# Reordering the first stage of a fused attention and MLP kernel, and the first two block products of its later groups

## The chip, the cores and the metric

The kernel runs on one core of a Trainium2 chip. The time is device time in microseconds, the median of several runs. A profile is one more execution, recorded by the hardware profiler; times inside it count from its first instruction. PE is the matrix engine, with PEld its weight loads; DVE, ACT and POOL are the vector, scalar and GpSimd engines; SP issues most DMAs. Each engine works through its own instructions in order and waits on semaphores for the others.

## The reference

Blockwise linear attention with a decay per head feeds a two-layer MLP with a norm and a residual:

```python
for b in range(nb):                       # 12 blocks of 64 rows, 4 batches, 8 heads of 64
    intra = einsum('bhic,bhjc->bhij', qb, kb) * Dmask
    intra = einsum('bhij,bhjd->bhid', intra, vb)
    inter = einsum('bhid,bhde->bhie', qb * lam_pow, kv_state)
    out[:, :, sl] = intra + inter
    kv_state = lam_block * kv_state + einsum('bhsd,bhse->bhde', kb * rev_pow, vb)
x = out.transpose(0, 2, 1, 3).reshape(4, 768, 512)
xn = (x - mean(x)) / sqrt(var(x) + 1e-6) * g_ln
return x + relu(xn @ w_ch1) @ w_ch2       # w_ch1 512x2048, w_ch2 2048x512
```

## The kernel before

**Windows.** The 3072 rows are cut into 12 windows u of 256 rows; window u belongs to batch u mod 4. A window has a first and a second 128-row chunk, `ab` = 0 and 1. k(u), q(u) and v(u), 512 KB each, are loaded by SP (L76); window 0's in two halves. `in_k` (L215, L231) casts k to bf16, `in_q_one(u, engine, j)` (L236) casts half j of q and scales it, `in_v` (L242) does so for v into `vb`. `transpose_pe(u, a, pairs)` (L250) turns k (a=0) or q (a=1) on PE into `kqT`; DVE or ACT copies it out of PSUM (L251). `scores` (L273), `mask` on DVE (L283), `kv` (L307), `new_state`, `av` (L419) and `inter` (L432) are the attention; `norm` (L465 to L470) reads the result `po` and leaves the centred `xc`; `keep_x` (L475) copies `po` to `x`; `to_xT(u, ab)` (L493) transposes `xc`; `rstd_of` (L506) makes the scale that is used only where the MLP's result is added. `sqrt_first` is a small activation that makes ACT load its square root table early.

**The MLP.** Each window is a group g of two 128-row tiles. Layer 1 takes W1 in four pieces `w1[c]` of 512 columns, layer 2 takes W2 in four pieces `w2[c]` of 512 rows; both are loaded and cast by DMAs that POOL issues (`load_w1` L117, `load_w2` L120). `m1a.tile(0, i)` and `m1b.tile(0, i)` (L640) apply W1(0) to one tile of group 0 or 1; `m1s(m1a, c, lo, hi)` (L530) applies halves of piece c to both tiles. Each result passes ReLU on ACT into `hT` (L533, L643). Groups 0 to 3 use the plain layer 2 (`m2`, L666, ended by `finish` L690). Groups 4 to 11 use seven products of half-size blocks (`m2w`, L624), with sums of W2 blocks (`w_sums`) and of hT blocks (`h_sums`, L548 to L550) made on DVE. A product has 8 multiplies r = 0 to 7 (L565) and adds into a PSUM bank; `evict` reads a bank when its product is complete.

**The order.** It is written out by hand; a step's instructions go to each engine's queue in the order in which the steps stand. `behind(tile)` (L727) is a one-column copy on POOL: it makes all that POOL issues after it wait for the DMA of that tile. `open_in(u, True)` writes one column of the k tile from POOL (L91), and SP's load of k(u) waits for it, with all that SP issues later. `mm_tile` gives one of four PSUM banks, the one free for longest. `units(n)` runs the next n entries of a plan: the rest of group 1's layer 1, then layer 2 of groups 0 and 1, then the later groups.

In the first stage (L736 to L998) POOL's steps stand in this order:

```python
    behind(qkv_in[0]["k"][:, 0, 0, 0:1]); load_w1(0); in_k(0, nc.gpsimd, HB)
    in_v(0, nc.gpsimd, HA); in_v(0, nc.gpsimd, HB)
    behind(qkv_in[1]["k"][:, 0, 0, 0:1]); load_w1(1); load_w1(2)
    in_q_one(1, nc.gpsimd, 0); in_q_one(1, nc.gpsimd, 1); load_w1(3); load_w2(0)
    in_v(1, nc.gpsimd); behind(w1[2][:, 0, 0:1]); open_in(2, True)
    behind(w2[0][:, 0, 0:1]); load_w2(1); load_w2(2)
    in_q_one(2, nc.gpsimd, 0); in_q_one(2, nc.gpsimd, 1); load_w2(3); in_v(2, nc.gpsimd); open_in(3, True)
```

PE's in the same stage, after `inter(0, 0)`: k(1)'s transposes, xT(0,0), inter(0,1), tile a(0,0), xT(0,1), q(1)'s transposes, tile a(0,1), scores of window 1, one m1 step, kv(1), two m1 steps, av(1), inter(1,0), m1, inter(1,1), m1, xT(1,0), m1, xT(1,1), tiles b(0,0) and b(0,1).

Of the kernel before, what the change touches and what calls it, by code (L numbers as in the profile page):

```python
# [12 lines left out]
ACT = mybir.ActivationFunctionType  # L13
# [4 lines left out]
def kernel(  # L18
# [97 lines left out]
    def load_w1(c):  # L116
        nc.gpsimd.dma_start(w1[c], moe_w_ch1[:, c * W1C:(c + 1) * W1C].rearrange("(k p) f -> p k f", p=128))  # L117
# [115 lines left out]
    def in_q_one(u, eng, j):  # L233
        src = qkv_in[u]["q"].rearrange("p (a e) j d -> p a e j d", e=2)
        lq = (lam_q[:, :, j] if u < LB else lam_p[:, 0, :]).rearrange("p (a e) -> p a e", e=2)
        eng.tensor_tensor(part(1, st[u]["kq"], ALL)[:, :, :, j], src[:, :, :, j],  # L236
                          lq[:, :, :, None].to_broadcast([128, NP, 2, D]), op=ALU.mult)

    def in_v(u, eng, hs=ALL):
        n = hs.stop - hs.start  # L240
        lv = lam_v[:, hs, :, None] if u < LB else lam_p[:, 1, hs, None, None]
        eng.tensor_tensor(st[u]["vb"][:, hs], qkv_in[u]["v"][:, hs], lv.to_broadcast([128, n, 2, D]), op=ALU.mult)  # L242
# [272 lines left out]
    def mlp(g):  # L515
# [38 lines left out]
        def product(i, bank, part, first):  # L554
            if first:
                pr[bank] = mm_tile([128, DM // 2], F32, f"pw{bank}")
            w, h = DM // 2, blocks()
            lhs = dict(P1=lambda r: h[:, r, 0], P2=lambda r: h[:, r, 2], P3=lambda r: hs["4"][:, r], P4=lambda r: h[:, r, 3],
                       P5=lambda r: hs["13"][:, r, 1], P6=lambda r: hs["2"][:, r], P7=lambda r: hs["13"][:, r, 0])[i]
            org = dict(P1=(0, 0), P2=(1, 0), P3=(1, 1)).get(i)  # L560
            own = dict(P5=0, P6=1, P7=2, P4=3).get(i)
            for r in part:
                c, k = divmod(r, W2K // 2)
                rhs = wt[c][:, k, own] if org is None else w2[c][:, 2 * k + org[0], org[1] * w:(org[1] + 1) * w]
                nc.tensor.matmul(pr[bank], lhsT=lhs(r), rhs=rhs, start=(first and r == 0), stop=(r == KB // 2 - 1),  # L565
                                 skip_group_check=True)
# [3 lines left out]
        def evict(i):  # L570
            u = g
            x, rstd = x_keep[u]
            w = DM // 2
            r = [rstd[:, ab:ab + 1] for ab in range(2)]
            xq = [[x[:, ab, z * w:(z + 1) * w] for z in range(2)] for ab in range(2)]

            def scaled(out, in0, ab, in1):
                nc.vector.scalar_tensor_tensor(out, in0=in0, scalar=r[ab], in1=in1, op0=ALU.mult, op1=ALU.add)  # L578

            def tmp(name):  # L580
                ev[name] = wk.tile([128, w], F32, tag="ev_" + name, bufs=1, name="ev_" + name)
                return ev[name]

            if i == "P1":
                o_of[u] = x
            o = o_of[u]
            oq = [[o[:, ab, z * w:(z + 1) * w] for z in range(2)] for ab in range(2)]
            if i == "P1":
                nc.scalar.activation(tmp("u1"), pr["a"], ACT.Identity, scale=r[0])  # L589
                nc.gpsimd.tensor_tensor(oq[0][0], ev["u1"], xq[0][0], op=ALU.add)  # L590
            elif i == "P2":
                scaled(oq[0][0], pr["b"], 0, oq[0][0])
                if u == NU - 1:
                    for j in range(2):
                        nc.sync.dma_start(rows_of(u)[j][:, 0, 0:w], o[half[j], 0, 0:w])
            elif i == "P7":
                nc.scalar.activation(tmp("p7"), pr["c"], ACT.Identity, scale=r[1])
                nc.gpsimd.tensor_tensor(xq[1][1], ev["p7"], xq[1][1], op=ALU.add)  # L598
            elif i == "P5":
                scaled(xq[1][1], pr["d"], 1, xq[1][1])  # L600
            elif i == "P6":
                scaled(o[:, 1].rearrange("p (z w) -> p z w", z=2), pr["a"][:, None, :].to_broadcast([128, 2, w]), 1,
                       x[:, 1].rearrange("p (z w) -> p z w", z=2))
                last_rows(1, 1)
                scaled(oq[0][1], pr["a"], 0, xq[0][1])
            elif i == "P4":
                scaled(oq[1][0], pr["c"], 1, oq[1][0])
                last_rows(1, 0)
            elif i == "P3":
                scaled(oq[0][1], pr["d"], 0, oq[0][1])  # L610
                last_rows(0, 1)

        def last_rows(ab, z):
# [4 lines left out]
            for j, eng in enumerate((nc.sync, nc.scalar)):  # L618
# [2 lines left out]
        products = (("P1", "a", True), ("P2", "b", True), ("P7", "c", True), ("P5", "d", True),  # L621
                    ("P6", "a", False), ("P4", "c", False), ("P3", "d", False))

        def m2w(n):  # L624
            lo, hi = 7 * n, 7 * n + 7
            for q, (i, bank, first) in enumerate(products):
                part = [r for r in range(8) if lo <= 8 * q + r < hi]
                if part:
                    product(i, bank, part, first and part[0] == 0)
                    if part[-1] == 7:  # L630
                        evict(i)

        def m1_tile(c, i):
            nonlocal hT
# [114 lines left out]
    for i in range(2):  # L749
        nc.scalar.activation(lam_p[:, i], lnlam, ACT.Exp, scale=e_p[:, i:i + 1])  # L750
    in_q(0, nc.vector, HA)
    behind(qkv_in[0]["k"][:, 0, 0, 0:1])
    load_w1(0)
    in_k(0, nc.gpsimd, HB)
    in_q(0, nc.vector, HB)
    transpose_pe(0, 1, (0, 1))
    transpose_pe(0, 0, (2, 3), nc.vector)
# [184 lines left out]
    in_k(1, nc.scalar)  # L942
    norm(0, 0, early=True)
    reader(0)
    behind(qkv_in[1]["k"][:, 0, 0, 0:1])
    load_w1(1)
    load_w1(2)
    in_q_one(1, nc.gpsimd, 0)
    in_q_one(1, nc.gpsimd, 1)
    load_w1(3)  # L950
    load_w2(0)
    in_v(1, nc.gpsimd)
    behind(w1[2][:, 0, 0:1])
# [12 lines left out]
    transpose_pe(1, 1, (0, 1), nc.vector)
    transpose_pe(1, 1, (2, 3))
    m1a.tile(0, 1)
    keep_x(0, nc.vector.tensor_copy)
    nc.scalar.activation(sqrt_first, eps_t, ACT.Sqrt)  # L970
    scores(1, 0)
    scores(1, 1, early=True)
    mask(1, 0)
    mask(1, 1)
    m1s(m1a, 1, 0, 1)
    kv(1, "sc")
    new_state(1, 0, nc.scalar)
    m1s(m1a, 1, 1, 2)
    rstd_of(0)
    m1s(m1a, 2, 0, 1)  # L980
    av(1, (0, 1))
    av(1, (2, 3))
    inter(1, 0)
    norm(1, 0, early=True)
    m1s(m1a, 2, 1, 2)
    inter(1, 1)
    norm(1, 1, early=True)
    st[1]["tmp"] = state_sum(1, 1)
    m1s(m1a, 3, 0, 1)
    to_xT(1, 0)  # L990
    m1s(m1a, 3, 1, 2)
    to_xT(1, 1)
    open_window(2)
    in_k_one(2, nc.vector, 0)
    in_k_one(2, nc.vector, 1)
    m1b.tile(0, 0)
    m1b.tile(0, 1)
    keep_x(1, nc.scalar.copy)  # L998
    rstd_of(1)
    behind(w2[0][:, 0, 0:1])  # L1000
    load_w2(1)
    load_w2(2)
    in_q_one(2, nc.gpsimd, 0)
    in_q_one(2, nc.gpsimd, 1)
    load_w2(3)
    in_v(2, nc.gpsimd)
    open_in(3, True)
    load_in(3, "k", nc.sync)
    load_in(3, "q", nc.sync)
# [347 lines left out]
```

## Time and profile before

| | |
|---|---|
| median of 3 runs | 210.56 us (210.29, 210.56, 211.72) |
| span of the profiled execution | 209.7 us |
| PE busy | 198.0 us, 94% |
| DVE, ACT, POOL busy | 137.1, 120.1, 85.1 us |
| layer 1, L530 | 736 multiplies, 84.8 us |
| W1 and W2 pieces | 8 DMAs of 512 KB each as written, 9.2 us from issue to landing (median) |
| loads of a whole k, q, v | 512 KB each, 6.2 to 8.2 us |

The page's picture of the span in 40 slices, each digit a tenth of busy time in that slice:

```profile
PE   2989599999999999999999999999999999999992
POOL 4746338229638240617255441781284202011020
DMA  4999999999899998992898998897978020058403
```

A slice is 5.2 us. PE is below nine tenths in the first, third, fifth and last slices alone (2, 8, 5, 2); the DMA engines are full from the second slice on for most of the run.

### The profile page before, as it was taken

Reading aid. Unit: us, or ns where it says so; the run is one execution under the profiler, and the core shown is the slowest. Engines: PE = TensorE matmul, PEld = TensorE weight load, DVE = VectorE, ACT = ScalarE, POOL = GpSimd, SP = SyncE. Lnnn points to the kernel's source line nnn. Section 1 sums busy time; section 2 is a strip of 40 time slices with the busy share of each in tenths; the row PEclk is TensorE's granted clock in tenths of the full one; section 3 lists DMA queues with packets and bytes.
Section 4 is the critical chain, followed back from the end, with each engine's and each line's share of the span. In section 5 each row is a group of like instructions: output and inputs, shape, how many; then the busy total and the mean of one; then the engine's idle time right before and its main releaser. Section 6 shows DMA issues by size and latency. Waiting matters only on the chain.

```text
span 209.7 us, 7231 instructions
## 1 busy us (share of the span) xinstructions
PE 198.0 (94%) x3099; PEld 156.6 (75%) x3099; DVE 137.1 (65%) x277; ACT 120.1 (57%) x277; POOL 85.1 (41%) x116
## 2 busy tenths in 40 slices
PE   2989599999999999999999999999999999999992
PEld 0469479645685577578888888888888888888881
DVE  2677481437575966749798775778777947865253
ACT  4764668516155468438666775485596575652620
POOL 4746338229638240617255441781284202011020
PEclk9999999999999999999999999999999999999998
DMA  4999999999899998992898998897978020058403
GB/s 121 294 270 211 206 276 167 196 306 273 159 322 201 218 184 159 194 271 55 177 226 124 187 204 155 201 208 109 226 134 185 6 50 3 18 125 279 137 14 88
DMA packets 91042, 36.39 MB, mean 174 GB/s; under 512 B 65153, under 2 KB 88193, under 8 KB 91010
## 3 DMA queue, kind: packets, MB, share of 16 engines
q1 hardware_dynamic: 86400, 31.53, 70.2%
q0 software_dynamic: 4224, 4.19, 12.6%
q8 instruction: 24, 0.39, 0.9%
q10 hardware_dynamic: 386, 0.20, 0.4%
q14 instruction: 8, 0.07, 0.1%
HBM read 27.27 MB, written 6.29 MB: 160 GB/s over the span
## 4 chain that ended last, share of the span: by engine, by line
PE 76%; DMA 7%; issue 7%; SPq 3%; DVE 3%; POOL 2%; POOLq 0%; ACT 0%; ACTq 0%; DVEq 0%
PE pm L530 34%; PE pm L666 14%; DMA vin<-in_v_dram 7%; PE pwa L565 6%; PE pwd L565 5%; PE pwc L565 5%; SPq L76 3%; PE pwb L565 2%; PE po L419 2%; PE po L432 1%; PE sc L273 1%; DVE x L578 1%; PE po L406 1%; PE sc L353 1%; PE pk L307 1%
## 5 line engine op out<-in xcount | busy, mean ns | idle before, releaser
L530 PE MATMUL pm<-xT,w 128*128 128x256 bf16 x736 | 84.8, 273 | 0.0
L530 PEld LDWEIGHTS <-w 128*128 128x128 bf16 x736 | 70.4, 98 | 9.5 <-DVE Smid L388 0.3
L533 ACT ACTIVATE hT<-pm 128x512 f16<-128x512 f32 x92 | 53.8, 598 | 28.8 <-PE pm L530 28.5
L666 PE MATMUL pm<-w,hT 128*128 128x512 f16 x128 | 30.2, 380 | 0.0
L565 PEld LDWEIGHTS <-hs 128*128 128x128 f16 x256 | 24.9, 98 | 2.9
L313 POOL TENSOR_TENSOR Sn<-Stmp,lam_s 128x256 bf16<-128x256 f32 x16 | 9.8, 615 | 42.1 <-DVE Stmp L317 23.6
L590 POOL TENSOR_TENSOR x<-ev_u,x 128x256 f32<-128x256 f32 x8 | 6.5, 816 | 45.0 <-ACT ev_u L589 45.0
L548 DVE TENSOR_TENSOR hs<-hT 128x1024 f16<-128x1024 f16 x16 | 12.8, 802 | 16.0 <-ACT hT L533 16.0
L565 PEld LDWEIGHTS <-hT 128*128 128x128 f16 x192 | 18.1, 98 | 3.6 <-ACT hT L533 1.6
L666 PEld LDWEIGHTS <-hT 128*128 128x128 f16 x128 | 11.7, 98 | 12.1
L283 DVE TENSOR_TENSOR mA<-sc,keep 128x512 bf16<-128x512 f32 x20 | 13.1, 684 | 7.0 <-PE sc L273 7.0
L458 ACT ACTIVATE x<-po 128x512 f32<-128x512 f32 x18 | 10.6, 590 | 9.7 <-PE po L419 5.3
L460 DVE SCALAR_TENSOR_TENSOR xc<-po,nmean,g_row 128x512 bf16<-128x512 f32 x18 | 12.9, 745 | 4.7 <-ACT nmean L459 4.7
L242 POOL TENSOR_TENSOR vb<-vin,lam_v 128x1024 bf16<-128x1024 f32 (+1 forms) x7 | 11.6, 1656 | 4.1 <-DMA vin<-in_v_dram 4.0
L503 ACT ACTIVATE sq<-x,nmean 128x512 bf16<-128x512 f32 x18 | 12.9, 719 | 0.3
L242 POOL TENSOR_TENSOR vb<-vin,lam_p 128x1024 bf16<-128x1024 f32 x6 | 11.9, 1985 | 2.5 <-DMA vin<-in_v_dram 2.5
L578 DVE SCALAR_TENSOR_TENSOR x<-pwd,rstd,x 128x256 f32<-128x256 f32 x16 | 7.7, 483 | 7.8 <-POOL x L598 7.8
L236 POOL TENSOR_TENSOR kq<-qin,lam_q 128x512 bf16<-128x512 f32 x10 | 10.3, 1045 | 5.6 <-DMA qin<-in_q_dram 5.6
L550 DVE TENSOR_TENSOR hs<-hs,hT 128x512 f16<-128x512 f16 x16 | 10.1, 628 | 0.6
L494 ACT COPY xT<-xt 128x512 bf16<-128x512 bf16 x10 | 5.8, 582 | 7.7 <-PE xt L493 7.7
L236 POOL TENSOR_TENSOR kq<-qin,lam_p 128x512 bf16<-128x512 f32 x9 | 9.3, 1042 | 1.3 <-PE pwc L565 1.2
L578 DVE SCALAR_TENSOR_TENSOR x<-pwa,rstd,x 128x512 f32<-128x512 f32 (+1 forms) x16 | 9.1, 613 | 0.8
(129 smaller groups left out, 300.4 us busy)
## 6 DMA issues: line engine op xcount, KB each, us to landing
out_dram<-x SPq DMA_DIRECT2D x22, 256.0 KB, 3.8
w<-in_moe_w_ch_dram POOLq DMA_DIRECT2D x8, 512.0 KB, 9.2
kin<-in_k_dram SPq DMA_DIRECT2D x14, 256.0 KB, 4.8
qin<-in_q_dram SPq DMA_DIRECT2D x14, 256.0 KB, 4.9
vin<-in_v_dram SPq DMA_DIRECT2D x14, 256.0 KB, 5.2
kin<-in_k_dram SPq DMA_DIRECT2D x5, 512.0 KB, 6.2
qin<-in_q_dram SPq DMA_DIRECT2D x5, 512.0 KB, 8.2
vin<-in_v_dram SPq DMA_DIRECT2D x5, 512.0 KB, 8.1
```

What stands on the lines that cost most here:

```text
L236: eng.tensor_tensor(part(1, st[u]["kq"], ALL)[:, :, :, j], src[:, :, :, j], lq[:, :, :, None].to_broadcast([128, NP, 2, D]), op=ALU.mult)
L242: eng.tensor_tensor(st[u]["vb"][:, hs], qkv_in[u]["v"][:, hs], lv.to_broadcast([128, n, 2, D]), op=ALU.mult)
L283: nc.vector.tensor_tensor(s[f"mA{hf}"][:, e], s[f"sc{hf}"][e], kp[:, None, :, :].to_broadcast([128, 2, 2, 128]), op=ALU.mult)
L458: nc.scalar.activation(x, po, ACT.Copy, accum_out=sm)
L460: nc.vector.scalar_tensor_tensor(xc, in0=po, scalar=nm, in1=g_row, op0=ALU.add, op1=ALU.mult)
L503: nc.scalar.activation(sq, s["x"][:, ab], ACT.Square, bias=s["nmean"][:, ab:ab + 1], accum_out=ss[:, ab:ab + 1])
L530: nc.tensor.matmul(pm[:, b, :], lhsT=w1[n // W2K][:, kk, (n % W2K) * 128:(n % W2K + 1) * 128], rhs=xT_of[g][:, kk, 0:N], start=(b == 0 and ...
L533: nc.scalar.activation(hT[:, u * NB:(u + 1) * NB, 0:N], pm, ACT.Relu)
L548: nc.vector.tensor_tensor(s13, b[:, :, 1:2, :].to_broadcast([128, n, 2, 128]), b[:, :, 0:4:3, :], op=ALU.subtract)
L565: nc.tensor.matmul(pr[bank], lhsT=lhs(r), rhs=rhs, start=(first and r == 0), stop=(r == KB // 2 - 1), skip_group_check=True)
L578: nc.vector.scalar_tensor_tensor(out, in0=in0, scalar=r[ab], in1=in1, op0=ALU.mult, op1=ALU.add)
L666: nc.tensor.matmul(acc[i], lhsT=hT[:, kk, i * 128:(i + 1) * 128], rhs=w2[kk // W2K][:, kk % W2K, :], start=(kk == 0), stop=(kk == KB - 1))
```

## The change

Five edits, all of order, but for two POOL copies that go (`behind` of k(0) and of k(1)) and some copies that move from one engine to another.

In the first stage POOL casts k(0) ahead of W1(0), and the W1 pieces stand between the casts of window 1. W2(0) goes behind the gate of window 2's loads; window 2's q casts go ahead of W2(1), its v ahead of W2(3). PE's order, q(1)'s transposes and the scores first, changes with it; q(1)'s transposes are copied out by ACT alone, and `keep_x(0)` moves from DVE to ACT. The table load and both `rstd_of` move past the second scores of window 2. In `m2w` the first two products take turns by seven multiplies.

```diff
+        early = [(q, r) for q in (0, 1) for r in range(7)] + [(0, 7), (1, 7)]
+        order = early + [(q, r) for q in range(2, 7) for r in range(8)]
+
         def m2w(n):
-            lo, hi = 7 * n, 7 * n + 7
-            for q, (i, bank, first) in enumerate(products):
-                part = [r for r in range(8) if lo <= 8 * q + r < hi]
-                if part:
-                    product(i, bank, part, first and part[0] == 0)
-                    if part[-1] == 7:
-                        evict(i)
+            for q, r in order[7 * n:7 * n + 7]:
+                i, bank, first = products[q]
+                product(i, bank, [r], first and r == 0)
+                if r == 7:
+                    evict(i)
...
     in_q(0, nc.vector, HA)
-    behind(qkv_in[0]["k"][:, 0, 0, 0:1])
+    in_k(0, nc.gpsimd, HB)
     load_w1(0)
-    in_k(0, nc.gpsimd, HB)
     in_q(0, nc.vector, HB)
...
     reader(0)
-    behind(qkv_in[1]["k"][:, 0, 0, 0:1])
+    in_q_one(1, nc.gpsimd, 0)
     load_w1(1)
+    in_q_one(1, nc.gpsimd, 1)
     load_w1(2)
-    in_q_one(1, nc.gpsimd, 0)
-    in_q_one(1, nc.gpsimd, 1)
+    in_v(1, nc.gpsimd)
     load_w1(3)
-    load_w2(0)
-    in_v(1, nc.gpsimd)
     behind(w1[2][:, 0, 0:1])
     open_in(2, True)
     load_in(2, "k", nc.sync)
     load_in(2, "q", nc.sync)
     load_in(2, "v", nc.sync)
+    load_w2(0)
     transpose_pe(1, 0, (0, 1), nc.vector)
     transpose_pe(1, 0, (2, 3), nc.vector)
     to_xT(0, 0)
     inter(0, 1)
     norm(0, 1, early=True)
     st[0]["tmp"] = state_sum(0, 1)
+    transpose_pe(1, 1, (0, 1))
+    transpose_pe(1, 1, (2, 3))
     m1a.tile(0, 0)
     to_xT(0, 1)
-    transpose_pe(1, 1, (0, 1), nc.vector)
-    transpose_pe(1, 1, (2, 3))
+    scores(1, 0)
+    mask(1, 0)
+    scores(1, 1, early=True)
+    mask(1, 1)
+    keep_x(0, nc.scalar.copy)
     m1a.tile(0, 1)
-    keep_x(0, nc.vector.tensor_copy)
-    nc.scalar.activation(sqrt_first, eps_t, ACT.Sqrt)
-    scores(1, 0)
-    scores(1, 1, early=True)
-    mask(1, 0)
-    mask(1, 1)
-    m1s(m1a, 1, 0, 1)
     kv(1, "sc")
     new_state(1, 0, nc.scalar)
-    m1s(m1a, 1, 1, 2)
-    rstd_of(0)
-    m1s(m1a, 2, 0, 1)
+    m1s(m1a, 1, 0, 1)
     av(1, (0, 1))
     av(1, (2, 3))
     inter(1, 0)
     norm(1, 0, early=True)
-    m1s(m1a, 2, 1, 2)
+    m1s(m1a, 1, 1, 2)
     inter(1, 1)
     norm(1, 1, early=True)
     st[1]["tmp"] = state_sum(1, 1)
+    m1s(m1a, 2, 0, 1)
+    to_xT(1, 0)
+    m1s(m1a, 2, 1, 2)
     m1s(m1a, 3, 0, 1)
-    to_xT(1, 0)
+    to_xT(1, 1)
     m1s(m1a, 3, 1, 2)
-    to_xT(1, 1)
     open_window(2)
     in_k_one(2, nc.vector, 0)
     in_k_one(2, nc.vector, 1)
+    in_q_one(2, nc.gpsimd, 0)
+    in_q_one(2, nc.gpsimd, 1)
     m1b.tile(0, 0)
     m1b.tile(0, 1)
     keep_x(1, nc.scalar.copy)
-    rstd_of(1)
     behind(w2[0][:, 0, 0:1])
     load_w2(1)
     load_w2(2)
-    in_q_one(2, nc.gpsimd, 0)
-    in_q_one(2, nc.gpsimd, 1)
+    in_v(2, nc.gpsimd)
     load_w2(3)
-    in_v(2, nc.gpsimd)
     open_in(3, True)
...
-    units(1)
+    units(2)
     transpose_pe(2, 0, (0, 1, 2, 3))
-    units(2)
+    units(1)
     transpose_pe(2, 1, (0, 1, 2, 3))
...
     units(2)
     s2(2)
+    nc.scalar.activation(sqrt_first, eps_t, ACT.Sqrt)
+    rstd_of(0)
+    rstd_of(1)
     units(2)
     s0(2)
```

More of the change, by code (lines that the diff above doesn't have):

```diff
@@ L1031, in units @@
             f(*a)
+    units(2)
+    transpose_pe(2, 0, (0, 1, 2, 3))
     units(1)
-    transpose_pe(2, 0, (0, 1, 2, 3))
-    units(2)
     transpose_pe(2, 1, (0, 1, 2, 3))
```

## The prediction

> **What bounds the kernel now.** I read the page first: TensorE (PE) is busy 94% of a 209.7 us span, so only its idle time is for sale. The table of stretches says where that is (columns: time and number of instructions for PE, weight loads, DVE, ACT, POOL, then clock, DMA share, GB/s):
>
> ```profile
> 22.00:24.16 2.16, 0.00 (x0) 0.02 (x1) 1.32 (x3) 1.06 (x3) 1.95 (x2) 1.00 1.24 207
> 31.00:186.00 155.00, 154.97 (x2505) 122.03 (x2503) 107.34 (x205) 94.14 (x223) 66.97 (x82) 1.00 0.86 169
> ```
>
> From 31 us to 186 us PE has no gap (the modelled ends touch), and one hole, 2.16 us, stands at 22 us. Whatever PE gains before 31 us reaches the end, as long as nothing behind it comes late. The timeline of PE names the hole and its pace:
>
> ```profile
> 15.84 1.86 PE L640 MATMUL pm1t<-xT,w 128*128 128x128 bf16 x16 [0.32 <-ACT xT L494]
> 20.94 1.05 PE L530 MATMUL pm<-xT,w 128*128 128x256 bf16 x8
> 24.16 0.44 PE L307 MATMUL pk<-vb,kq 64*64 64x64 bf16 x32 [2.17 <-POOL vb L242]
> 30.94 1.95 PE L640 MATMUL pm1t<-xT,w 128*128 128x128 bf16 x32
> ```
>
> The hole waits for vb of window 1. Also, 16 multiplies take 1.86 us at 15.84 and 32 of the same take 1.95 us at 30.94: single records start 107 ns apart until 19.9 us, 56 ns after it. The early stage runs at half pace. Why vb is late, from POOL's timeline:
>
> ```profile
> 5.40 0.94 POOL L117 DMA_DIRECT2D w<-in_moe_w_ch_dram  x1
> 11.38 1.56 POOL L117 DMA_DIRECT2D w<-in_moe_w_ch_dram  x2
> 15.62 2.05 POOL L236 TENSOR_TENSOR kq<-qin,lam_q 128x512 bf16<-128x512 f32 x2 [2.68 <-DMA qin<-in_q_dram]
> 22.21 1.90 POOL L242 TENSOR_TENSOR vb<-vin,lam_v 128x1024 bf16<-128x1024 f32 x1 [3.05 <-DMA vin<-in_v_dram]
> ```
>
> POOL waits for q(1) until 15.6 and for v(1) until 22.2, although SP issued both by 9.3 us. The DMA queues by stretch, 3 to 9.5 us and then 9.5 to 13.5 us (packets, MB, share):
>
> ```profile
> q1 hardware_dynamic: 3750, 1.87, 109.6%
> ```
> ```profile
> q0 software_dynamic: 514, 0.51, 76.6%
> q1 hardware_dynamic: 861, 0.43, 44.1%
> ```
>
> q1 is SP's loads, q0 the weight pieces. Alone, q1 moves 1.87/6.5 = 0.288 MB/us; beside W1(0) it falls to 0.43/4 = 0.11. W1(0), issued at 5.40, first moves after 9.5. Last, the chain of waits, for the block products:
>
> ```profile
> 99.39 0.97 PE pwa L565 x8
> 100.36 0.87 PE pwb L565 x8
> ```
>
> Eight groups open with such a 0.97; the groups of instructions put 1.6 us, 8 times, of weight loads waiting for the last hT against them.
>
> **Part 1: W1(0) behind in_k(0).** The copy at 5.15 goes; POOL's casts of k stay at 6.95 (they wait for k) and end at 7.87; W1(0) issues 7.87 to 8.8, in the 0.93 us in which POOL waited for v anyway. So 2.5 us later. Its first packets came 3.5 us after the end of the issue (6.34, 9.9; W1(1): 12.20, some 15.6), so now about 12.3. Until then q1 is undisturbed: the loads up to q(1) are 2.62 MB, from 2.8 us at 0.288, so 11.9; completion counted 1.2 us later, as for k(0) (0.26 MB by 3.7, seen at 5.1): q(1) at 13.2 instead of 15.54. Bounds: 12.6, and 15.5 if W1(0) cuts in as it does now.
>
> The Trainium skill, DMA: Bandwidth & Descriptors, Specifications, gives the first byte of a gpsimd-issued DMA about 1 us, and its section on queues has each DMA engine take turns between queues packet by packet. By that W1(0) would move at 9.8 us, q(1) would come as late as now, and the kernel would take about 209.8. The row (3.5 us, twice) speaks for 12.3, and I go by the row.
>
> **Part 2: the new POOL order.** A cast of q half takes 1.04, a weight issue 0.81, vb 1.90. q cast 13.2 to 14.25, W1(1) to 15.05, q cast to 16.1, W1(2) to 16.9, then v(1). Behind the new first wait stand both W1 pieces, vb, W1(3) and the gate of window 2's loads. v(1) and W1(0) share the engines from 12.3: 1.05 MB at 0.94 per 4 us ends at 16.7, plus 1 us: v(1) at 17.7, vb at 19.6, W1(3) issued to 20.4. Weight pieces alone move 1.18 MB in 16 to 22 us, so 2.66 us each: data ends 19.3, 22.0, 24.7, landings with 1.2 us: 20.5, 23.2, 25.9. If W1(3) needs its 3.5 us after 20.4, 27.8.
>
> **Part 3: PE.** q(1)'s transposes are now ahead of the first tile: 8 of them, 0.95 (17.93 to 18.87), from 16.1; tile(0,0) 1.66, whose W1(0) takes 3.6 us from 12.3 (9.9 to 13.5 before) and 0.84 to land: 16.8 against 17.05; xT 0.43; 32 score multiplies 0.57 at full pace, about 1.2 at half, I take 0.9 (nearer neither: the pace changes about there); tile(0,1) 1.5. kv starts at 21.5, with vb there 1.9 us before. From kv to tile b(0,0) it was 30.94 - 24.16 = 6.78, of which 0.18 waited for xc (now 0: a norm has a whole m1 step more). One m1 step that stood before kv (0.87) now follows it: 21.5 + 6.60 + 0.87 = 29.0. W1 is needed at 21.9, 24.8 and 27.0 against 20.5, 23.2 and 25.9 to 27.8; I allow 0.2 of wait. Tile b at 29.2: lead 1.7 us. Bounds: 2.8 (clock up early, no wait) and -0.3 (q(1) at 15.5).
>
> The Trainium skill, TensorE: Matmul & The Clock Gate, Part 1, has full pace follow a free-running window of about 3.4 us of sustained work. That speaks against starving PE until 16.1; with full pace between 19.5 and 22.9, the lead moves by about 0.6 either way, which these bounds hold.
>
> **Part 4: what is late next.** W1(2) lands at 23.2 against a gate at 24.18 before, so k(2), q(2), v(2) issue some 0.5 us sooner, and are now ahead of W2(0). q(2) lands at about 30 to 32 (32.18 before), its casts end 32.1 to 34; PE wants them at 34.1 (35.79 - 1.7). Cost 0. W2(0) moves from 18.42 to about 24, lands 31 to 33.5, wanted at 37.8: 0. W2(1) and W2(2) wait for it and for the q casts: 34 instead of 29.77; the landing took 7.2 there, so 41.2; wanted at 42.90 - 1.7 = 41.2. Just covered; bounds 0 and the rival below. W2(3) 38 instead of 34.25, lands by 47, wanted at 47.9. POOL's memset for k(3) slips 1.4 us, but kqT(3) landed at 56.6 for scores at 71.3: 0.
>
> ACT takes 1.07 (keep_x) and 0.58 more, DVE 1.7 less; ACT has 5.5 us of work between 15.5 and 24: 0. The 1.28 us table load and both rstd go to ACT's 5.3 us idle time at 40 us, long before the finish at 51.45: 0. units(2)/units(1) swapped: same sum.
>
> **Part 5: block products.** With seven P1 and seven P2 products ahead of P1's last, its hT has 7 x 0.109 = 0.76 us to come against a wait of 0.10: 8 x 0.10 = 0.8 us gone. P1's eviction is 0.76 later; P6 writes its bank 17 products (1.85 us) after it instead of 2.6, and ACT's ev_u takes 0.48: 0. P5's eviction waits for P7's, as now. Bounds 0.4 to 0.8.
>
> **Sum.** 209.7 - 1.7 - 0.8 = 207.2 profiled; the median of the runs is 0.86 above the span, so 208.1.
>
> **Rivals.** *q(1) stays late:* W1(0) and q(1) overlap again. For: now they do, for 4 us. Against: W1(0) is issued after both q(1) and most of v(1). Lead -0.3 to 0.2: 209.8.
> *Slower: the W2 chain.* W2(1) waits on W2(0), which now follows W1(2)'s landing. Landings took 7.2 to 11.6 us from issue. With 11.6 for W2(0) (24.2 to 35.8) and the median 9.3 for W2(1): 45.3, 4.1 after 41.2: 208.1 + 4.1 = 212.2. It decides from a landing of W2(1) past 41.2, and ends slower than before past 43.7. Against: the long landings stood behind two or three other pieces, and at 34 us only v(2) is ahead.
> *The interleaving gives nothing:* another wait, say for a bank, replaces the 0.10. Then 208.9. Against: bank b's relu ended 1.7 us before its first product.
>
> **Numbers.** Forecast 0.64, q(1) late 0.17, W2 chain 0.12, no interleaving gain 0.07. About 1% (2.1 us) is what a measurement here can tell from no change. The forecast's own range is 206.8 to 209.0; three quarters of it (0.48) are under 208.45, 0.16 above. The third rival gives 0.02 faster and 0.05 same, q(1) late 0.16 same and 0.01 slower, the chain 0.06 same (it also covers smaller delays) and 0.06 slower. So faster 0.50, same 0.43, slower 0.07. The range, 206.8 to 211.0, leaves out the chain's upper part and an early clock.
>
> **What would show it.** POOL's first cast of q(1) at 13.2 (not 15.6); kv near 21.5 with no wait for vb; tile b at 29.2; L565's first eight at 0.87; no PE gap at 39 to 48 us. A wait of PE for a DMA of w, at 27 us or at 41 us, would break it, and so would q(1) at 15 us or later.

## The result and the profile after

| | before | after |
|---|---|---|
| median of 6 runs | 210.92 us (210.29 to 211.72) | 214.18 us (213.74 to 215.45) |
| ratio to before, 95% interval | | 1.0154 [1.0112, 1.0196] |
| span of the profiled execution | 209.7 us | 212.0 us |
| PE busy | 198.0 us | 198.5 us |

Ratios, unlike medians, leave out executions of more than 1.5% above the fastest of the same kernel.

The change costs 3.3 us where 2.5 us of gain were forecast, and the time lies outside the range. PE does the same 3099 multiplies in 0.5 us more busy time, so most of the loss is idle time. The table of stretches of the changed kernel says where (columns as before: time and instructions of PE, weight loads, DVE, ACT, POOL, then granted clock, DMA share, GB/s):

```profile
33.00:37.00 4.00, 3.22 (x38) 2.74 (x36) 0.00 (x0) 3.45 (x6) 3.60 (x5) 1.00 0.08 22
56.00:66.00 10.00, 7.73 (x122) 6.44 (x121) 9.43 (x13) 3.89 (x7) 8.04 (x10) 1.00 1.15 256
66.00:187.00 121.00, 120.94 (x2057) 99.64 (x2056) 89.21 (x173) 76.63 (x188) 47.71 (x62) 1.00 0.83 155
```

And the same two first stretches of the kernel before:

```profile
33.00:37.00 4.00, 4.00 (x46) 3.67 (x45) 0.17 (x1) 4.00 (x9) 3.98 (x6) 1.00 1.11 165
56.00:66.00 10.00, 10.00 (x213) 7.81 (x210) 6.54 (x15) 5.67 (x11) 4.75 (x6) 1.00 1.11 253
```

Two stretches that had no idle PE time now have it, 0.8 and 2.3 us. In the first the DMA engines stand empty (share 0.08, 1.11 before); in the second DVE and POOL are both fuller than before (9.43 and 8.04 of 10 us). Behind 66 us PE has no gap, as before. PE's timeline, the lines that answer to those of the prediction and every wait of over half a microsecond after 20 us:

```profile
21.11 0.66 PE L307 MATMUL pk<-vb,kq 64*64 64x64 bf16 x32
24.16 0.22 PE L419 MATMUL po<-vb,mA 64*64 64x64 bf16 x4 [0.80 <-issue]
29.61 1.95 PE L641 MATMUL pm1t<-xT,w 128*128 128x128 bf16 x32
35.51 0.56 PE L250 MATMUL tp<-ident,kq 128*128 128x128 bf16 x7 [0.78 <-POOL kq L236]
60.45 0.42 PE L273 MATMUL sc<-kqT 64*64 64x128 bf16 x16 [0.94 <-DMA kqT<-kq]
63.33 0.21 PE L273 MATMUL sc<-kqT 64*64 64x128 bf16 x1 [0.61 <-DVE mA L283]
64.26 0.41 PE L273 MATMUL sc<-kqT 64*64 64x128 bf16 x15 [0.72 <-DVE mA L283]
```

The hole at kv (24.16 before) is gone and tile b(0,0) starts 1.33 us sooner than in the profile before. Then four waits, at 35.51, 60.45, 63.33 and 64.26, take 3.05 us; before had none there, and reached the scores of window 3 at 59.59:

```profile
59.59 0.40 PE L273 MATMUL sc<-kqT 64*64 64x128 bf16 x16
```

Held against the profile before, the same multiplies are 1.33 us ahead at 29.6 us, 0.33 ahead from 38 to 49, 2.4 behind from 63 on, and 2.1 behind at the last product. POOL's timeline shows where the waits come from:

```profile
13.19 1.05 POOL L236 TENSOR_TENSOR kq<-qin,lam_q 128x512 bf16<-128x512 f32 x1 [2.21 <-DMA qin<-in_q_dram]
18.19 1.89 POOL L242 TENSOR_TENSOR vb<-vin,lam_v 128x1024 bf16<-128x1024 f32 x1 [1.39 <-DMA vin<-in_v_dram]
33.40 2.05 POOL L236 TENSOR_TENSOR kq<-qin,lam_q 128x512 bf16<-128x512 f32 x2 [9.28 <-DMA qin<-in_q_dram]
35.52 1.55 POOL L120 DMA_DIRECT2D w<-in_moe_w_ch_dram  x2
39.73 0.12 POOL L91 MEMSET kin<- 128x1 f32 x1
52.09 2.05 POOL L236 TENSOR_TENSOR kq<-qin,lam_q 128x512 bf16<-128x512 f32 x2 [7.80 <-DMA qin<-in_q_dram]
57.27 2.41 POOL L236 TENSOR_TENSOR kq<-qin,lam_q 128x512 bf16<-128x512 f32 x2
59.65 2.08 POOL L242 TENSOR_TENSOR vb<-vin,lam_v 128x1024 bf16<-128x1024 f32 x1
```

The lines of before that answer to 35.52, 39.73, 52.09 and 59.65:

```profile
29.77 1.55 POOL L120 DMA_DIRECT2D w<-in_moe_w_ch_dram  x2 [0.27 <-issue]
36.92 0.10 POOL L91 MEMSET kin<- 128x1 f32 x1
46.58 2.06 POOL L236 TENSOR_TENSOR kq<-qin,lam_q 128x512 bf16<-128x512 f32 x2 [1.95 <-DMA qin<-in_q_dram]
54.09 1.90 POOL L242 TENSOR_TENSOR vb<-vin,lam_v 128x1024 bf16<-128x1024 f32 x1
```

POOL stands 9.28 us at q(2), with nothing done since 24 us, and the issues of W2(1) and W2(2) stand behind that cast: 35.52, where they were at 29.77. W2(1) to W2(3) landed at 41.40, 44.85 and 49.17 (36.96, 40.19 and 43.15 before). The gate of k(3) went from 36.92 to 39.73, k(3) landed at 50.16 and q(3) at 51.96 (46.45 before), and POOL's casts of windows 3 and 4 start at 52.09 instead of 46.58. From there two waits follow: kqT(3), which the DMA transposes now deliver at 60.41 (56.64 before), is late for scores that PE reaches at 59.5; and the casts of window 4 run on to 61.7 instead of 56.0, beside the sums of W2 blocks on DVE:

```profile
57.63 1.15 DVE L790 TENSOR_TENSOR wt<-w,wt 128x512 f16<-128x512 f16 x1
58.81 1.15 DVE L791 TENSOR_TENSOR wt<-wt,w 128x512 f16<-128x512 f16 x1
59.89 2.12 DVE L787 TENSOR_TENSOR wt<-w 128x512 f16<-128x512 f16 x1
61.93 0.41 DVE L788 TENSOR_TENSOR wt<-w 128x512 f16<-128x512 f16 x1
```

All six sums took 0.41 or 0.42 us before, when POOL's cast had ended at 55.99, ahead of the first of them. The line of before for the sum at 59.89:

```profile
58.19 0.42 DVE L787 TENSOR_TENSOR wt<-w 128x512 f16<-128x512 f16 x1
```

The one of 2.12 us ends at 62.01, just after the POOL cast that began at 59.65 (61.73). The masks of window 3 queue behind the sums, and PE waits for them at 63.33 and 64.26.

The interleaving did what it was to do. In the groups of instructions, the block products' weight loads of hT have 2.2 us of idle time ahead of them, none put against ACT's hT (3.6 before, 1.6 of it for hT); before, then after:

```profile
L565 PEld LDWEIGHTS <-hT 128*128 128x128 f16 x192 | 18.1, 98 | 3.6 <-ACT hT L533 1.6
L565 PEld LDWEIGHTS <-hT 128*128 128x128 f16 x192 | 18.8, 98 | 2.2
```

### The profile page after: what moved, and what is told of

The parts are those of the page before. It is cut to its first block, busy times and chain, and to the rows that moved or that the text cites. A ratio compares the mean times of both kernels' runs of the same rounds, so it can differ in the third digit from the quotient of the medians.

```text
span 212.0 us, 7226 instructions
## 1 busy us (share of the span) xinstructions
PE 198.5 (94%) x3099; PEld 157.6 (74%) x3099; DVE 135.9 (64%) x274; ACT 121.8 (57%) x280; POOL 84.0 (40%) x114
## 4 chain that ended last, share of the span: by engine, by line
PE 74%; DMA 11%; DVE 6%; POOL 3%; SPq 2%; issue 1%; POOLq 0%; ACT 0%; DVEq 0%
PE pm L530 32%; PE pm L667 13%; DMA qin<-in_q_dram 8%; PE pwd L565 6%; PE pwc L565 6%; PE pwa L565 6%; DMA w<-in_moe_w_ch_dram 3%; PE pwb L565 3%; SPq L76 2%; POOL kq L236 2%; PE po L432 1%; PE po L419 1%; DVE wt L787 1%; DVE x L578 1%; PE sc L273 1%; PE po L406 1%
## 5 line engine op out<-in xcount | busy, mean ns | idle before, releaser
L530 PE MATMUL pm<-xT,w 128*128 128x256 bf16 x736 | 84.8, 273 | 0.0
L530 PEld LDWEIGHTS <-w 128*128 128x128 bf16 x736 | 70.5, 98 | 9.4 <-DVE Smid L388 0.3
L590 POOL TENSOR_TENSOR x<-ev_u,x 128x256 f32<-128x256 f32 x8 | 5.8, 727 | 50.0 <-ACT ev_u L589 38.6
L667 PEld LDWEIGHTS <-hT 128*128 128x128 f16 x128 | 11.7, 98 | 12.1
L565 PEld LDWEIGHTS <-hT 128*128 128x128 f16 x192 | 18.8, 98 | 2.2
L565 PE MATMUL pwa<-w,hT 128*128 128x256 f16 x64 | 9.6, 273 | 0.0
```

What stands on the lines that cost most here:

```text
L530: nc.tensor.matmul(pm[:, b, :], lhsT=w1[n // W2K][:, kk, (n % W2K) * 128:(n % W2K + 1) * 128], rhs=xT_of[g][:, kk, 0:N], start=(b == 0 and ...
L667: nc.tensor.matmul(acc[i], lhsT=hT[:, kk, i * 128:(i + 1) * 128], rhs=w2[kk // W2K][:, kk % W2K, :], start=(kk == 0), stop=(kk == KB - 1))
```

## The experiments

"Changed" and "before" are the two kernels. Each time stands beside runs of before on the same chip; the ratio carries the interval. e1 to e4 ran on one chip, b2 and e5 to e14 on a second, e15 and e16 on a third, so across these groups compare ratios.

| run | edit | median us | before us | ratio, 95% | span of the profile |
|---|---|---|---|---|---|
| b2 | before, once more, one run | 210.94 | | | 209.2 |
| e1 | changed, all W2 steps put back | 211.67 | 210.50 | 1.0049 [1.0031, 1.0067] | 209.7 |
| e2 | changed, W2(0) alone put back | 214.35 | 210.50 | 1.0139 [1.0072, 1.0205] | 212.6 |
| e3 | changed, q and v casts of window 2 put back | 211.70 | 210.50 | 1.0054 [1.0031, 1.0077] | 210.3 |
| e4 | before with the new W2 order | 214.50 | 210.50 | 1.0153 [1.0085, 1.0221] | 212.4 |
| e5 | before with the interleaved products | 210.16 | 211.28 | 0.9956 [0.9924, 0.9987] | |
| e7 | changed, three sums later | 214.57 | 211.28 | 1.0177 [1.0121, 1.0232] | 212.1 |
| e8 | before with the early part alone | 212.10 | 211.30 | 1.0046 [1.0021, 1.0071] | 210.5 |
| e9 | e1, W1 and W2(0) ahead of v(1)'s cast | 212.47 | 211.30 | 1.0047 [1.0012, 1.0081] | 209.8 |
| e10 | e1, window 2 let go at W1(1) | 211.75 | 211.30 | 1.0040 [1.0018, 1.0063] | 210.0 |
| e11 | e9 and e10 together | 213.08 | 211.30 | 1.0086 [1.0051, 1.0121] | 211.4 |
| e12 | e1, W2(0) held behind k(2) | 211.02 | 211.12 | 0.9993 [0.9964, 1.0022] | 209.2 |
| e13 | e5, W2(0) held behind k(2) | 210.06 | 211.12 | 0.9949 [0.9918, 0.9980] | 208.2 |
| e14 | e5 again | 210.09 | 211.12 | 0.9948 [0.9917, 0.9979] | 208.4 |
| e15 | e13, v(4)'s cast later | 210.66 | 210.66 | 0.9967 [0.9930, 1.0005] | 208.4 |
| e16 | e5, v(4)'s cast later | 210.93 | 210.66 | 0.9978 [0.9941, 1.0015] | 210.1 |

### Which of the W2 steps costs it: e1, e2, e3, e4

The theory (A): POOL's wait for q(2) in front of W2(1) to W2(3) makes the loss. The rival (B): the early reorder makes the later loads late by itself.

e1 puts the W2 steps back where before had them; e2 moves W2(0) alone (the first two stretches of the diff), e3 the casts alone (the last two), and e4 is the reverse of them all, made in the kernel before.

```diff
     load_w1(3)
+    load_w2(0)
     behind(w1[2][:, 0, 0:1])
...
     load_in(2, "v", nc.sync)
-    load_w2(0)
...
-    in_q_one(2, nc.gpsimd, 0)
-    in_q_one(2, nc.gpsimd, 1)
     m1b.tile(0, 0)
...
     load_w2(2)
-    in_v(2, nc.gpsimd)
+    in_q_one(2, nc.gpsimd, 0)
+    in_q_one(2, nc.gpsimd, 1)
     load_w2(3)
+    in_v(2, nc.gpsimd)
```

e1: 

> The changed kernel with POOL's steps from W2(0) on in the old order (W2(0) ahead of the gate of window 2's loads, window 2's q casts behind W2(2), its v behind W2(3)). Theory A, that the new W2 order costs it all (q(2) beside W2(0), W2(1) to W2(3) and window 3's loads late, then kqT(3) and the masks of window 3 late): the three stalls at 35.5, 60.5 and 63 to 64 us go, the lead of 1.3 us at tile b and the 0.5 us of the block products stay: about 209.0 against 210.9 before. Theory B, that the earlier steps (W1 among the casts, q(1)'s transposes first) make the later loads late by themselves: it stays at 212 or more, with kqT(3) landing past 59.6 us.

e2: 

> The changed kernel with only W2(0) put back ahead of the gate; window 2's q casts still stand ahead of W2(1) on POOL. If the sharing of the engines between W2(0) and q(2) is what counts, q(2) lands by 32 us, W2(1) is issued by 34.3 (35.5 changed) and the time is 209.5 to 210.5. If the place of the q casts ahead of W2(1) counts more, W2(1) still issues past 35 us, kqT(3) lands past 59.6 us and the time stays above 212.5.

e3: 

> The changed kernel with W2(0) still behind the gate, but window 2's q casts back behind W2(2) and its v cast behind W2(3). If the q casts ahead of W2(1) count: W2(1) issues at 32.2 us (W2(0) lands at 31.9), the gap of the DMA engines at 34 to 37 us closes, window 3's loads come 1.4 to 3 us earlier, PE still waits about 1 us for q(2) at 35 to 36 us, but not for kqT(3) at 60: about 211.0 to 211.8. If the place of W2(0) counts alone: 213.5 or more.

e4: 

> The kernel before, with the new W2 order alone (W2(0) behind the gate, window 2's q casts ahead of W2(1), its v ahead of W2(3)). Theory A: kqT(3) lands about 60.5 us against a need of 59.6, the sums of W2 blocks on DVE meet POOL's casts of window 4, the masks come late: 212.5 to 214. Theory B: 210.5 to 211.5, no PE gap at 60 us.

e1 and e3 lose the 2.5 us at once, and e1 has no PE wait from 37 to 70 us; e2 changes nothing (on the same chip it is 2.7 us slower than e1). So it is the casts of window 2 ahead of the W2 issues, and not the place of W2(0): in e3 W2(1) is issued at 32.21, and kqT(3) lands at 58.30, still ahead of its scores. e4 gives the other half of the proof: put into the kernel before, that order alone costs 1.0153, as much as the whole change and a little more than expected, with three of its four waits (PE's timeline of e4):

```profile
35.59 0.56 PE L250 MATMUL tp<-ident,kq 128*128 128x128 bf16 x7 [0.78 <-POOL kq L236]
61.08 0.42 PE L273 MATMUL sc<-kqT 64*64 64x128 bf16 x16 [1.57 <-DMA kqT<-kq]
64.35 0.41 PE L273 MATMUL sc<-kqT 64*64 64x128 bf16 x15 [0.71 <-DVE mA L283]
```

B is out for these 2.5 us: e1 keeps the early reorder, and its kqT(3) lands at 57.78. But theory A expected 209.0 of e1, which came to 211.67: without the W2 edits the change is still 0.5% slower than before. Why is asked below.

### The sums beside POOL's casts: e7, e15, e16

e7 moves three pairs of sums behind the last norm of window 3, out of the way of its masks.

```diff
     units(5)
-    w_sums(0, 0)
-    w_sums(0, 1)
     units(2)
-    w_sums(1, 0)
     units(1)
     s1(3)
...
     s4(3)
+    w_sums(0, 0)
+    w_sums(0, 1)
+    w_sums(1, 0)
```

> The changed kernel with the sums of the first W2 blocks on DVE moved behind window 3's attention (from before its scores to after its last norm). If those sums, slowed beside POOL's casts, are what makes window 3's masks late: PE's waits at 63.3 and 64.3 us go, the one for kqT(3) at 60.5 stays, and the time falls by 1.0 to 1.6 us to about 212.8. If the masks are late because the scores are: no change, 214.

The waits at 63 and 64 us go and PE is 1.29 us ahead of the changed kernel at 65 us. The six sums, now at 68.9 to 74.8 us, then delay window 4's masks: new waits of 0.50 us at 75.89 and 0.94 at 77.04. The gain is given back, and the time is the same instead of the 212.8 us expected. This one later place saves nothing; what is left to save is the sums' slowness.

e15 and e16 ask what makes them slow, by moving one cast of POOL's out from beside them (e15 on top of e13, e16 on top of e5).

```diff
     in_q_one(4, nc.gpsimd, 1)
-    in_v(4, nc.gpsimd)
     units(5)
...
     s1(3)
+    in_v(4, nc.gpsimd)
```

e15: 

> The kernel before with interleaved products and W2(0) held behind k(2), and the v cast of window 4 (POOL, 1.9 us) moved from ahead of the W2 sums to behind the new state of window 3. Theory L (a sum on DVE stands still while a POOL cast runs): all six sums at 54 to 59 us take 0.41 to 0.45 us instead of one of 2.12, the mask of window 3 starts 1.7 us sooner, PE's wait of 0.70 us at 60.87 is gone, the time falls by 0.7 to 0.9 us, to 209.2 to 209.5, unless window 5's casts, 1.9 us later on POOL, hold PE at 70 to 80 us. Theory N (the sums are slow by themselves, for instance because W2(0) or the banks are busy): one sum is still over 1.5 us, the wait stays, 210.0.

e16: 

> The kernel before with interleaved products alone, and the same move of the v cast of window 4. Theory L: the sum of 1.54 us at 55.5 becomes 0.41 to 0.45 us; PE had no wait of over 0.25 us at 60 us in that profile, so the time falls by 0 to 0.2 us only, 209.8 to 210.1. Theory N: the sum stays over 1.2 us and the time is 210.0 to 210.1.

DVE's timeline of e13, and after it that of e15:

```profile
54.76 0.57 DVE L788 TENSOR_TENSOR wt<-w 128x512 f16<-128x512 f16 x1
55.25 2.12 DVE L789 TENSOR_TENSOR wt<-w 128x512 f16<-128x512 f16 x1
57.40 0.42 DVE L791 TENSOR_TENSOR wt<-w,wt 128x512 f16<-128x512 f16 x1
```
```profile
55.02 0.44 DVE L788 TENSOR_TENSOR wt<-w 128x512 f16<-128x512 f16 x1
55.39 0.41 DVE L789 TENSOR_TENSOR wt<-w 128x512 f16<-128x512 f16 x1
55.84 0.43 DVE L791 TENSOR_TENSOR wt<-w,wt 128x512 f16<-128x512 f16 x1
```

In e13 POOL's v cast runs from 55.00 to 57.08, and the sum that begins in it ends at 57.37. With the cast gone each of these six sums takes 0.41 to 0.44 us, in e16 too, and PE's wait of 0.70 us at 60.87 in e13 is gone in e15. Theory L holds: such a sum stands still until the running cast ends. The time did not follow: e15 is 0.69 us ahead of e13 until 94 us, then shows a new PE wait of 0.62 us at 95.33, for which the trace names no releaser, and is 0.1 behind from there on. Where the wait came from was not tried; a wait of the same kind stands at 24 us (below). Neither run is told from the kernel without its edit, and both missed the times expected of them.

### The interleaved products alone: e5, e14

The edit is the change's own hunk in `m2w`, made in the kernel before.

e5: 

> The kernel before with the new order of the first two block products alone. If each of the eight groups loses its wait of 0.10 us and nothing else comes in: 0.5 to 0.8 us less, ratio 0.996 to 0.998 (the changed kernel's lag fell by about 0.5 us over these groups). If the later eviction of P1 costs it elsewhere: ratio 1.000 or more.

e14: 

> The kernel before with the interleaved block products alone, again: 0.9 us less than before (ratio 0.9956 in the first run), with a profile. In it the first-eight wait of the block products is gone, and PE's offset to the kernel before falls by about 0.1 us in each of the last groups, 0.7 us by the last product.

Both runs gain 0.4 to 0.5%, 0.9 to 1.1 us; their intervals together hold 0.3 to 1.8. e5's profiled execution spans 684 us and isn't read, so e14 was run; in it PE gains on b2 by about 0.1 us in most of the last groups, from 0.35 us ahead at 95 us, in front of the first block product, to 0.84 at the last one. The gain is real; its size lies between the trace's 0.5 and the times' 1.1, and the prediction's 0.8 is among them.

### Why the early part gains nothing: b2, e8 to e13

b2: 

> The kernel before, profiled once more: its runs have spans of 208.3 to 209.3 us, the profile at hand 209.7. Where does the difference lie? If in the early stage: vb of window 1 and kv earlier than 24.16 us, or the full pace of PE earlier than 19.9; the work after 36 us the same to 0.1 us.

e8 is e1 with the old order of products, which leaves the early part alone.

> The change with its early part alone: W1 pieces, casts, transposes and scores of the second pair as in the changed kernel, but the old order of the W2 loads and the old order of the block products. Theory W (a wall: the q casts of window 2 end at 35 to 36 us whatever the early part gains, because q(2) lands behind the W1 pieces, and W1(3), W2(0) are issued 2 to 3 us later than before): no gain is left and the wall is 1 us later, so it is the version with all W2 loads back (211.67) plus the 0.9 us of the interleaving: 212.4 to 212.8, ratio to before about 1.009. Theory G (the early part does give its 1.3 us or more, and the old order of products hides nothing): 210.0 to 210.5, ratio at or under 1.000. Under W the trace has a PE wait of about 1 us at 35 to 36 us, and k(2), q(2) land at about 32.3 and 34.0.

By its time the early part costs 0.5%, which lies between the two theories. That e1, with the interleaving on top, has no better ratio is not what theory W expected; e8's trace does fall behind e1's in the late groups, from 0.15 us ahead at 38 us to 0.61 behind at the last product, and the medians differ by 0.4 us, so I take it that the interleaving works there too and that the runs of before differ from chip to chip (210.5 and 211.3). No run tests this.

Three findings bear on the early part. The first is in the executions. Start of kv(1) and of tile b(0,0) in each profile:

| | kv(1), us | tile b(0,0), us |
|---|---|---|
| before's early order: before, b2, e14, e16 | 24.16, 22.72, 22.09, 24.82 | 30.94, 30.34, 29.65, 31.77 |
| changed early order: after, e1, e2, e3, e7, e8, e10, e12 | 21.11 to 22.44 | 29.52 to 30.46 |
| before's early order, W2(0) later: e4, e13, e15 | 22.39, 21.80, 22.01 | 29.46, 29.10, 29.36 |

The 2.17 us for vb, on which the forecast rested, stands in one of the four. Against the four's mean (30.7) the changed order (mean 29.9) is 0.8 us sooner, not 1.7. Half of that is one execution again: e16's multiplies keep the half pace until 25.3 us (eight of L530 take 1.89 us at 23.00 and 1.05 at 27.99), and without it the mean is 30.3. The half pace ends at 19.7 to 22.0 us in the eight profiles of the changed order, at 18.6 to 20.0 in the other six. And where W2(0) alone is out of the way, before's own order is as early as any.

The second is that the changed order has waits of its own: in after 0.38 us for POOL's q cast at 16.12 and 0.80 at 24.16, in e1 0.51 for the cast, 0.43 for W1(0) and 0.72 at 24.44. The wait at 24 us stands inside av, and the trace names no releaser for it (`<-issue`). It is not for the masks of window 1, which av reads; the last one ended at 22.47 in after (DVE's timeline):

```profile
21.19 1.28 DVE L283 TENSOR_TENSOR mA<-sce,keep 128x512 bf16<-128x512 f32 x2
```

It falls ahead of the same multiply each time, av's 61st in six profiles of the changed order and its 44th in three of before's, and in all of them it ends 1.3 to 1.5 us after a 16 KB packet of the instruction queue, q8, has ended: 24.16 after 22.69 in after, 24.63 after 23.20 in e12, 26.14 after 24.82 in b2 (and 95.33 after 93.89 for the wait in e15). In none of the 17 profiles read does that multiply start sooner than 1.3 us after the packet, and in all eight of the changed order tile b(0,0) starts 5.45 us behind it. This fits PE waiting there for its own next instructions, which would hold tile b however early kv is. No run tests it.

The third is q(2). PE cannot pass its transposes before POOL has cast it, and in e1 that ends at 36.1 us (PE's timeline of e1):

```profile
35.17 0.23 PE L250 MATMUL tp<-ident,kq 128*128 128x128 bf16 x1 [0.26 <-POOL kq L236]
36.17 0.56 PE L250 MATMUL tp<-ident,kq 128*128 128x128 bf16 x7 [0.78 <-POOL kq L236]
```

q(2) landed at 33.99 there, 32.18 to 33.16 in the profiles of before and b2. e9, e10 and e11 try to bring it sooner by order alone:

```diff
     reader(0)
-    in_q_one(1, nc.gpsimd, 0)
     load_w1(1)
+    in_q_one(1, nc.gpsimd, 0)
     in_q_one(1, nc.gpsimd, 1)
     load_w1(2)
-    in_v(1, nc.gpsimd)
     load_w1(3)
     load_w2(0)
+    in_v(1, nc.gpsimd)
```
```diff
-    behind(w1[2][:, 0, 0:1])
+    behind(w1[1][:, 0, 0:1])
     open_in(2, True)
```

e9 (the first): 

> The version with all W2 loads back, and on POOL the W1(1) load issued ahead of the first q(1) cast (POOL is idle there from 11.16 to 13.36), and W1(2), W1(3), W2(0) all ahead of the v(1) cast. Theory W: W1(3) and W2(0) no longer wait for the v(1) cast (issued 17 to 19 instead of 20.5 to 22.1), the weight stream runs without its gap at 23 to 25.5 us, q(2) lands at 32.0 to 32.8 instead of 33.99, the two PE waits of together 1.04 us at 35 to 36 us shrink to under 0.4: 210.4 to 211.0 us, ratio about 0.998 to 1.000. Theory R (the rest of the kernel, not the landing of q(2), sets the pace after 36 us): 211.5 to 211.8, as without the edit.

e10 (the second): 

> The version with all W2 loads back, with one size changed: POOL lets the loads of window 2 go when W1(1) has landed (21.1 us) instead of W1(2) (23.8 us). Theory W: k(2), q(2), v(2) are issued 1 to 2.7 us sooner (POOL is busy until 22.06) and land 1 to 2 us sooner, q(2) at 32.0 to 33.0 instead of 33.99, sharing engines with W1(3) and W2(0), which land later by about as much; the PE waits at 35 to 36 us (1.04 us together) shrink to 0 to 0.4, and the time is 210.6 to 211.2 us, unless W1(3) is then late for its tiles (a new PE wait at 28 to 33 us). Theory R: 211.5 to 211.8.

e11 (both): 

> Both edits together: the weight stream moved ahead of the v(1) cast, and window 2 let go when W1(1) has landed. Theory W: q(2) lands at 31 to 32.3, the PE waits at 35 to 36 us are gone and the lead of about 1.3 us at the first tile of the second pair is kept past 40 us, unless W2(0) or W2(1) is then late: 209.6 to 210.6 us, ratio 0.994 to 1.000. Theory R: 211.5 to 211.8.

In e10 k(2) was issued 2.07 us sooner (22.04) and landed no sooner (32.40 against 32.29), nor q(2) (34.14): the engines had W1(3) and W2(0) to move too. In e9 q(2) landed at 32.67 and the waits at 35 us went, as expected; but all pieces from W1(1) to W2(0) were now issued before v(1) had landed, and the hole at kv is back (POOL's timeline of e9, then PE's):

```profile
22.03 1.90 POOL L242 TENSOR_TENSOR vb<-vin,lam_v 128x1024 bf16<-128x1024 f32 x1 [4.50 <-DMA vin<-in_v_dram]
```
```profile
23.98 0.45 PE L307 MATMUL pk<-vb,kq 64*64 64x64 bf16 x32 [1.64 <-POOL vb L242]
```

From 38 us on e9's multiplies run at the same times as e1's, to 0.1 us. The profiled execution took 211.53 us, 0.9 less than the median of e9; the difference goes with the clock (below). e11 is e9's hole again, and its profiled execution lost another 1.5 us to the clock. In these three runs order only chose who waits: theory W's mechanism is seen, its gains are not.

e12 takes bytes away from in front of q(2) instead, and e13 does so without the early part:

```diff
     load_w1(3)
-    load_w2(0)
     behind(w1[2][:, 0, 0:1])
...
     load_in(2, "v", nc.sync)
+    behind(qkv_in[2]["k"][:, 0, 0, 0:1])
+    load_w2(0)
+    load_w2(1)
...
-    behind(w2[0][:, 0, 0:1])
-    load_w2(1)
-    load_w2(2)
     in_q_one(2, nc.gpsimd, 0)
     in_q_one(2, nc.gpsimd, 1)
+    load_w2(2)
     load_w2(3)
```

e12: 

> The version with all W2 loads back (early part and interleaving kept), with the W2(0) load held until k(2) has landed and W2(1) behind it, so that 0.5 MB less goes ahead of q(2); W2(2) and W2(3) are issued behind the q casts of window 2. Theory D (the DMA engines are busy without a gap to 37 us, so what goes ahead of q(2) decides): q(2) lands at 30.0 to 31.5 instead of 33.99, the two PE waits of 1.04 us together at 35 to 36 us are gone, W2(0) lands at 34 to 36 (first read at 39.7), W2(3) at 42 to 44, no new wait at 60 to 65: about 1.0 us less than 211.67, 210.4 to 210.9, ratio 0.998 to 1.001. Theory P (the lead is lost in PE's own work): q(2) lands sooner but the time stays at 211.5 to 211.9. If W2(0) or W2(1) is late, a wait at 39 to 44 us on w shows it.

e13: 

> The kernel before with the interleaved block products and the same hold of W2(0) behind k(2), but without the early part. Theory D: before has no PE wait for q(2) in its profiles (q(2) at 32.2 to 33.2, casts done by 34 to 35.2), so q(2) at 29.5 to 30.5 gains 0 to 0.2 us: the ratio stays that of the interleaving alone, 0.994 to 0.997, and if the early part is worth its lead then the run without it is slower than the one with it by up to 1.3 us. Theory P: the same time here, and the one with the early part slower than this by about 1 us.

POOL's and PE's timelines of e12:

```profile
31.06 2.05 POOL L236 TENSOR_TENSOR kq<-qin,lam_q 128x512 bf16<-128x512 f32 x2 [0.92 <-DMA qin<-in_q_dram]
```
```profile
33.62 0.61 PE L250 MATMUL tp<-ident,kq 128*128 128x128 bf16 x8
34.94 0.61 PE L250 MATMUL tp<-ident,kq 128*128 128x128 bf16 x8
```

q(2) lands at 30.98, no wait is left at 35 us, and the ratio falls from e1's 1.0049 to 0.9993 (0.65 us by the medians, 1.2 by the ratios): theory D, which expected 1.0 us. So the bytes ahead of q(2) were the wall. But e13, without the early part, is 0.96 us faster still, on the same chip, which is what theory P expected of it: with the wall gone, the early part is worth less than nothing. At 37 us e12's multiplies are 1.0 us behind e13's, with waits of 0.51, 0.42 and 1.01 us at 16.2, 17.6 and 24.6 us (q cast, W1(0), and the one without a releaser) against 0.32 and 0.28 us in e13. Neither e13's hold of W2(0) nor e14 without it beats the other; both, 210.06 and 210.09, beat before and the changed kernel.

## Why the prediction was wrong

**Parts 1 and 2 were right as events.** q(1) landed at 13.12 (13.2 forecast), vb was ready at 20.08 (19.6), W1(1) to W1(3) landed at 20.49, 23.15 and 25.71 (20.5, 23.2, 25.9). On the rule weighed there, of the Trainium skill, DMA: Bandwidth & Descriptors, Specifications: W1(0)'s first packets came 2.7 us after the end of its issue (11.62 after 8.91; 3.2 before), not about 1, and q(1) was not disturbed. The row was nearer.

**Part 3 was near, from a wrong base.** kv at 21.11 (21.5), tile b at 29.61 (29.2), and the full pace at 19.8 us, within the 19.5 to 22.9 weighed there; the term left out is the 0.80 us at 24.16, which the trace puts to nobody. But the 1.7 us were counted against one execution, and that was not a typical one. The sum's last term shows it: the time of a run is 1.7 us above its span in each profile whose run time is known (211.44 and 209.7 in e1, 210.94 and 209.2 in b2, 210.07 and 208.4 in e14). So the profiled execution of before took about 211.4 us, 0.9 above the 210.56 that the forecast started from and 0.5 above the median of six, and "0.86 above the span" laid a late execution's span to a median run. The hole for vb was that execution's own.

**Part 4 failed, in three places, and this is the step that made the prediction wrong.** "Cost 0" for q(2): PE wanted it before it was cast, and waited 0.78 us; the same wall stood close behind before's early stage. "For scores at 71.3: 0": those are window 4's scores. Window 3's are reached at 59.6, so kqT(3), landed at 56.6, had 3.0 us of slack and not 14.7, and k(3) slipped 2.8 us at its gate (1.4 forecast) and 5.5 by the cast, as W2(1) to W2(3) were late ahead of it. And nothing was priced for where POOL's own casts would come to lie when they move by 5.5 us: on the W2 sums. Where the forecast had 0 for the new W2 order, e1 and e4 put it at 2.5 us and 3.2 us (1.0153).

**The slower rival had the place and not the victim.** W2(1) landed at 41.40 against the 41.2 from which that rival decides, and PE has no gap from 39 to 48 us. W2(3) came nearest: landed at 49.17 it cost 0.1 us, and in e2, landed at 49.93, 0.43. The delay went past W2 to what is loaded behind it. (That rival's 35.8 and 9.3 add to 45.1 and not 45.3, and in Part 1 k(0)'s 3.7 and 5.1 lie 1.4 apart and not 1.2; neither decides anything.)

**Part 5 was right in its mechanism**, and its size is within the noise: 0.8 forecast, 0.9 and 1.1 by the times, 0.5 by the traces (in the changed kernel too, 2.56 us behind before at 95 us and 2.08 at the last product).

**The sum again, with what the runs gave.** Early part +1.0 (e8, 1.0046) for -1.7, W2 order +3.2 (e4) for 0, products -0.9 to -1.1 for -0.8: +3.1 to +3.3, and +3.3 was measured. That it comes out so close is partly luck: these are edits made one at a time, and on top of one another they are worth something else, 2.2 to 2.7 for the W2 order (after and e2 against e1) and 0 to 0.4 for the products (e1 against e8).

## What to carry to other kernels

When a waiting instruction is moved up on a queue that issues loads, follow each load that it now holds to its last reader, window after window, and name that reader by its index: the nearest reader was just covered here, and the third one paid. With the DMA engines full, as here, issuing a load sooner did not land it sooner (e10); what went ahead of it had to become less (e12). And before a hole in one profile is taken for the price, a second profile of the same kernel, or the run's time against its span, tells whether the hole is there as a rule.

## What the runs showed of the hardware

**Sums on DVE stand still during a cast on POOL.** A sum with two f16 inputs takes 0.41 us alone; begun during a POOL cast, it ends 0.28 or 0.29 us after that cast, whatever is left of it: 62.01 after 61.73 in the changed kernel, 57.37 after 57.08 in e13, 57.50 after 57.21 in e12, 57.02 after 56.73 in e14. In e15 and e16, with the cast away, none of these six is over 0.44, and a later sum that began beside window 5's cast shows the same again: 67.42 after 67.14 and 69.82 after 69.54. DVE's casts of k do it too: in b2 the one at 49.43 takes 2.12 us and ends 0.28 after POOL's cast (51.27), in the changed kernel, with POOL idle, each takes 0.42 or 0.43.

The Trainium skill, SBUF — State Buffer, Who interferes with whom, says that a VectorE instruction with two SBUF inputs contends with a GpSimd instruction that reads SBUF; it calls the ports that they share an exclusive lock, and says of VectorE's 2-port mode that whoever issues first has them for the whole instruction while the other fully blocks. For the sums the runs agree, with these numbers.

**A clock lost in the first stage.** In e11's profiled execution PE stood idle for 1.85 us ahead of 24.15 us, and the granted clock fell to a half after it, from 25.5 to 28.9 us:

```profile
24.00:26.00 2.00, 1.85 (x76) 1.53 (x79) 0.00 (x0) 1.32 (x5) 0.26 (x3) 0.87 1.23 207
26.00:28.00 2.00, 2.00 (x59) 1.57 (x52) 1.10 (x4) 0.21 (x1) 0.00 (x0) 0.50 1.19 278
28.00:30.00 2.00, 2.00 (x23) 1.44 (x22) 1.52 (x4) 0.62 (x2) 1.07 (x3) 0.77 1.08 309
```

Its multiplies are 1.5 us behind e9's from there to the end. e9's hole of 1.64 us at the same place cost no clock in its profiled execution, nor did before's of 2.17, so a hole there may cost more than its length, and not in every execution. The runs say the same: six of e9's twelve and six of e11's eleven have a mean granted clock of 0.987 to 0.992, and these took 212.68 us or more in e9 and 213.05 or more in e11; in e1, e8, e12, e13 and e14 none of 58 runs is under 0.995. That the hole is what brings it on is likely, but no run shows it.
